# One load queue with casts on the engines, and head-major query features for eight 64x32 array tiles

**Chip, cores, metric.** One core of one Trainium2 chip. The metric is the device time of one execution in microseconds (us). A profiled execution also has a *span*, from the first to the last instruction, which lies about 2.1 us under the time. A ratio below is the mean time of one kernel's fast runs over that of the other's fast runs of the same rounds, so it is not quite the ratio of the medians quoted beside it; a "fast" run is one within about 1.5% of its kernel's fastest.

Names used throughout: PE is the tensor engine, PEld its weight loads, DVE the vector engine, ACT the scalar engine, POOL GpSimd, SP the engine that issues most transfers. In the traces, H holds `x @ w_in` before the silu (two buffers), G its silu (eight buffers), Vh a batch's values as bf16, `ot` a transposed block of the output. The "key-value products" of a batch are the `kv` of the reference, its "numerators" the `num`. A line of a profile's timeline gives start, duration, engine, line of the program, operation, tiles (written<-read), shapes, how many were merged, and in brackets the idle time before it and what ended it.

## The reference

Linear attention with quadratic features, then an expert layer with silu. 4 batches, 4 heads, 1088 positions, head dimension 32.

```python
def phi(x):                       # 8 x 8 = 64 features of each position
    a = np.einsum('rd,bhsd->bhsr', S1, x)
    b = np.einsum('rd,bhsd->bhsr', S2, x)
    return np.einsum('bhsi,bhsj->bhsij', a, b).reshape(*x.shape[:-1], 64)
kv  = einsum('bhsf,bhsd->bhfd', phi(k), v);  z = sum_s phi(k)
num = einsum('bhsf,bhfd->bhsd', phi(q), kv)
den = einsum('bhsf,bhf->bhs',  phi(q), z)[..., None] + 1e-06
x   = (num / den), heads side by side          # 4352 tokens x 128
h   = x @ w_in                                 # 128 -> 2048
out = (h * sigmoid(h)) @ w_out                 # 2048 -> 128
```

## The kernel before

The program is a list of small tasks. A constant `ORDER` says in which order they are emitted and, where a task may run on several engines, on which. Each engine works its own part of that list strictly in order, and SP issues its transfers strictly in order. So a place in the list is as much a part of the kernel as the instruction. What the change touches:

```python
def load_in(i):     # w_in, cast to bf16 by the GpSimd queue's transfer
    nc.gpsimd.dma_start(w_in[:, DFF // 2 * i: DFF // 2 * (i + 1)], moe_w_in[:, DFF // 2 * i: DFF // 2 * (i + 1)])
def load_out(i):    # w_out likewise
    nc.gpsimd.dma_start(w_out[:, 8 * i: 8 * (i + 1), :].rearrange(...), moe_w_out[...].rearrange(...))
gate = pl.add("POOL", 0.1, lambda: nc.gpsimd.tensor_copy(out=mark, in_=Kx[0][...]), ...)  # holds them back till keys 0 are in
...
def kvm():          # duplicate K'V and mask it, so that two heads share one 128-row product
    nc.vector.tensor_tensor(out=st["kvx"], in0=_bc(st["kvp"][:, 0: R * R], 0, 2), in1=_bc(pmask[:, :], 1, R * R), op=ALU.mult)
...
def num(sl):        # numerators: block-masked KV, whole 128x128 array, two head pairs accumulate
    for hp in range(2):
        nc.tensor.matmul(sl[:, :m], kst["KV"][:, hp, :], rhs, start=(hp == 0), stop=(hp == 1))
```

SP's order was: second half of queries 0, first half, values 0, keys 1, one piece of values 2, keys 2, a piece of values 1, queries 1, another piece of values 1 and so on. Two of the four pieces of values 2 stand behind the transposes of batch 1's query features.

Of the kernel before, what the change touches and what calls it, by code (L numbers as in the profile page):

```python
# [15 lines left out]
ORDER = """  # L16
7 0 64 6 18 19 1 2.1 3.0 23 24 20 21 22 12 25 27 26 4 5 14 13 15 40 8 45 65 46 49 48 41 42 43 66 69
68 47 50 57 67 16.0 30.0 31 32.0 33 36.0 17.0 38.0 39 51 37 52.0 53 54.0 34.1 35 28.1 29 44.1 55
56.0 58 59.0 60 61.0 87 10 95 94 219 220 222 70 71 72.0 62 63.1 96 98 97 9 225 11 221 223 224 228
135 73 226 227 229 131 138 77.1 74.0 233 234 78 79.1 230 231 236 237 104 80 102.0 91 92 112 75 105  # L20
76.1 90 235 139 239 106 81.0 240 242 243 107 175 183 113 116 114 115 117 247 250 100.0 103.0 99.0
238 241 244 118 119.0 248 249 253 132 89 251 252 256 245 254 232 88 136 140 142 141 257 93.0 177
101.0 255 123.1 259 260 108 148 149 258 262 263 182 109 110 144.0 261 265 120 111.0 121 143.0 266
268 269 264 150 122.1 273 274 267 276 277 156 270 271 82.1 83 84.0 151 279 280 246 124 125 126.1
282 283 184 157 186 185 159 146.0 299 302 300 133 180 134 179 158 272 303 145.0 147.0 137.0 152 192
189.0 160 161 162 305 306 163.0 285 286 275 127.1 278 281 288 289 164 178 284 308 85 86.1 309 287
167.0 168 311 312 301 314 315 304 307 191.0 317 318 171.0 172 153 154 310 291 292 187.1 313 294 295
155.0 165 166.1 320 321 316 319 193 325 326 290 328 329 293 194 188.1 200 331 195 128 332 296 297
334 335 169 170.1 337 338 176 322 323 201 340 341 343 204 298 344 181.0 203 324 202 190.0 196 351
205 352 206 207.0 208 327 330 197 354 355 333 336 357 358 339 360 361 353 129 130.1 363 364 356 366  # L30
198 342 369 367 370 359 372 373 199.0 209 210.1 346 347 362 173 174.1 377 378 211.1 212 345 380 365
215.1 216 381 217 218.1 383 384 348 386 387 379 389 390 213 403 404 368 382 392 393 371 406 407 374
385 395 396 388 398 349 350 399 391 409 410 394 214.1 417 418 375 376 397 420 421 400 401 402 412
413 405 408 423 424 411 431 432 414 415 416 426 427 419 434 435 422 437 438 425 428 429 430 440 441
433 436 439 442 443 444
"""
# [8 lines left out]
class Plan:  # L45
# [29 lines left out]
    def replay(self, seq):  # L75
        now, mode, queue, port = dict(self.now), None, 4.0 - 1.6, 0.0
        free = {k: [(i, 0.0) for i in range(len(v))] for k, v in self.slots.items()}
        for t, c in seq:
            eng, cost = t["eng"][c], t["cost"][c]
            at = max(now.get(eng, 0.0), t["ready"])  # L80
            for d in t["deps"]:
                at = max(at, d["done"] + d["lag"] + self.hop(d["on"], eng) * (d["dq"] == 0.0))
            got = []
            for pool in t["take"]:
                i, when = free[pool].pop(0)
                got.append(i)
                at = max(at, when)
            if eng == "PE":
                cost += self.MODE if mode not in (None, t["mode"]) else 0.0
                mode = t["mode"]  # L90
            if t["tt"] and eng in ("DVE", "POOL"):
                at = max(at, port)
                port = at + cost
            t["on"], t["start"], t["end"], t["got"] = eng, at, at + cost, got
            now[eng] = t["done"] = t["end"]
            if t["dq"]:
                queue = t["done"] = max(queue, t["end"]) + t["dq"]
            for u, i in t["give"]:
                free[u["take"][i]].append((u["got"][i], t["end"] + self.FREE))
# [19 lines left out]
def kernel(  # L119
# [11 lines left out]
    nc = tc.nc  # L131
# [78 lines left out]
    QTs = [const.tile([P, 4, CW], FP32, name=f"QT{i}") for i in range(2)]  # L210
    KVs = [const.tile([P, 2, P], BF16, name=f"KV{i}") for i in range(2)]
    AW = [const.tile([P, NBX * H, R + 1], FP32, name=f"AW{i}") for i in range(2)]
# [6 lines left out]
    identb = const.tile([P, P], BF16, name="identb")  # L219
    mark = const.tile([P, 1, 1], FP32, name="mark")  # L220
    warm = const.tile([P, 1], FP32, name="warm")
# [16 lines left out]
    for t in Vf:  # L238
        nc.vector.memset(t[64:, :, NB, :], 0.0)
    for t in KVs:  # L240
        nc.gpsimd.memset(t, 0.0)
    for t in AW:
# [45 lines left out]
    def key_tasks(b, cuts):  # L288
# [65 lines left out]
        def kvm0(eng):  # L354
            st["KV"] = KVs[b % 2]
            dst = AP(tensor=st["KV"].tensor, offset=st["KV"].offset, ap=[list(st["KV"].ap[0]), [P + 64, 2], [D, 2], [1, D]])
            src = H0[:, :, 0:64].rearrange("p q (g d) -> p q g d", g=2)
# [16 lines left out]

        def kvm():
            st["kvx"] = work.tile([P, 2, R * R], BF16, name="kvx", tag="kvx")
            nc.vector.tensor_tensor(out=st["kvx"], in0=_bc(st["kvp"][:, 0: R * R], 0, 2),
                                    in1=_bc(pmask[:, :], 1, R * R), op=ALU.mult)

# [4 lines left out]
        def kvc(eng):  # L384
            st["KV"] = KVs[b % 2]
            dst = AP(tensor=st["KV"].tensor, offset=st["KV"].offset, ap=[list(st["KV"].ap[0]), [P + 64, 2], [1, 64]])
            copy(eng, dst, st["kvb"].rearrange("p (q m) -> p q m", q=2))

# [15 lines left out]
        for i, (lo, hi) in enumerate(parts):  # L404
# [3 lines left out]
                         (st["pr"][-1:] if False else []) + ([st["lk"]] if b else []) + old,  # L408
                         ready=((3.5, 3.95), (4.5, 4.9))[i][c // 2] if b == 0 else 0.0, name=nm(f"kt{c}{lo}")) for c in (0, 2)]
            st["kt"] += k1  # L410
# [27 lines left out]
        if b == 0:  # L438
            st["kvd"] = pl.add(("DVE", "ACT"), (0.3, 0.44), kvm0, kvs, name=nm("kvm"))
            early.append(st["kvd"])  # L440
        else:
            k1 = pl.add("PE", 0.42, kv, ou + vc, take=("s",), mode="32", name=nm("kv"))
            t = pl.add("DVE", 0.29, kvm, [k1], name=nm("kvm"))
            t = pl.add("PE", 0.12, kvt, [t], name=nm("kvt"))
            st["kvd"] = pl.add(("DVE", "ACT"), (0.22, 0.3), kvc, [t] + ([qs[b - 2]["nums"]] if b >= 2 else []),
                               give=[(k1, 0)], name=nm("kvc"))
# [19 lines left out]
    def scale_cost(n):  # L466
        return 0.75 + 0.13 * n

    def back_end(b, o, lo, hi, pe):
# [40 lines left out]
        m = pl.add("PE", 0.05 + 0.107 * n, num, [c, kst["kvd"]], take=("s",), name=nm("num"))  # L510
        st["nums"] = m
        st[f"x{lo}"] = pl.add(both, (0.17 + 0.107 * n, 0.08 + 0.135 * n), xcopy, [m], give=[(m, 0)],
                              due=T0 + STEP * (16 * b + 12) if n == 1 else None, name=nm("x"))

    def query_tasks(b, spans, pe=False, groups=None):
# [57 lines left out]
        for g, (glo, ghi) in enumerate(groups):  # L573
# [7 lines left out]
            for lo, hi in spans:  # L581
                if lo < glo or hi > ghi:
                    continue
                o = pl.add(("DVE", "POOL"), (0.1 + 0.26 * (hi - lo), 0.08 + 0.52 * (hi - lo)),
                           lambda e, lo=lo, hi=hi: outer(e, lo, hi), [sc], tt=True, name=nm(f"outer{lo}"))
                back_end(b, o, lo, hi, pe)

    def store_main(b, a0, na, queues):
# [103 lines left out]
    def load_in(i):  # L692
        nc.gpsimd.dma_start(w_in[:, DFF // 2 * i: DFF // 2 * (i + 1)], moe_w_in[:, DFF // 2 * i: DFF // 2 * (i + 1)])

    def load_out(i):
        nc.gpsimd.dma_start(w_out[:, 8 * i: 8 * (i + 1), :].rearrange("p (i j) m -> p i (j m)", i=2),
                            moe_w_out[DFF // 2 * i: DFF // 2 * (i + 1), :].rearrange("(i p j) m -> p i (j m)", i=2, p=P))

    gate = pl.add("POOL", 0.1, lambda: nc.gpsimd.tensor_copy(out=mark, in_=Kx[0][:, KN[0] + KN[1] + KN[2] + CUT: KN[0] + KN[1] + KN[2] + CUT + 1, 0:1]), ready=4.9, due=4.0, name="gate")
    for i in range(2):  # L700
        win += [dma(524, lambda i=i: load_in(i), [gate], issue=0.75, lag=2.6, due=4.2 + 0.1 * i, eng="POOL", rate=400.0, name=f"lwi{i}")] * 2
    for i in range(2):
        wout += [dma(524, lambda i=i: load_out(i), [gate], issue=0.85, lag=2.6, due=4.5 + 0.1 * i, eng="POOL", rate=380.0, name=f"lwo{i}")] * 2

# [8 lines left out]
    for b in range(1, B):  # L713
        pl.floor = T0 + 1.0
        load(b)
        key_tasks(b, KCUT)
        query_tasks(b, [(0, 4), (4, 8), (8, 9)])
    pl.floor = None
    for b in range(B):
        for lo, hi in ((0, 2), (2, 4), (4, 8)) if b == 0 else (  # L720
                ((0, 4), (4, 6), (6, 8)) if b == B - 1 else ((0, 4), (4, 8))):
            if (b, lo) == (B - 1, 4):
                moe_tasks(xR.rearrange("p b x -> p (b x)"), B * XN, [qs[i]["x8"] for i in range(B)], store_rest, 8, tag="mR")
            need = [qs[b][f"x{i}"] for i in range(8) if f"x{i}" in qs[b] and lo <= i < hi]
            need = need or [qs[b][f"x{i}"] for i in range(8) if f"x{i}" in qs[b] and i <= lo][-1:]
            moe_tasks(xT[b][:, P * lo: P * hi], P * (hi - lo), need,
# [39 lines left out]
```

## Time and profile before

| | before |
|---|---|
| time, first comparison | median 102.04 us (101.77 to 104.64, 4 runs) |
| time, three later comparisons, 11 runs each | medians 102.18, 101.74, 101.53 us (99.72 to 105.32) |
| first expert matmul in the trace | 17.58 us (second trace 16.81) |
| ACT silu, 68 instructions | 64.8 us busy, 7.7 us idle in front of them |
| last output transpose starts | 93.10 us (second trace 94.46) |

### The profile page before, as it was taken

What the parts mean: (1) busy time and instruction counts of PE and PEld (TensorE: products, weight loads), DVE (VectorE), ACT (ScalarE), POOL (GpSimd) and SP (SyncE); (2) the same over time, 40 slices, a digit from 0 to 9 for tenths busy, and PEclk for the clock granted to TensorE, in tenths of its full rate; (3) what the DMA queues carried; (4) which work ended last, traced back from release to release, by engine and by line L of the source; (5) the groups of instructions that cost most, each with busy time, mean ns of one, the idle gap of its engine ahead of it and who ended that gap; (6) DMA issues with size and microseconds to landing.
All of it is one profiled execution on the core that took longest, in us unless ns stands there. A gap on an engine that the chain in (4) does not pass through costs nothing.

```text
span 98.6 us, 2224 instructions
## 1 busy us (share of the span) xinstructions
PE 89.5 (91%) x852; PEld 52.5 (53%) x852; DVE 54.7 (55%) x135; ACT 72.0 (73%) x89; POOL 33.4 (34%) x43
## 2 busy tenths in 40 slices
PE   5996999999999799978999999999999999999700
PEld 4543476798573445425445453554444556899500
DVE  4563779998799927689691848791123220211200
ACT  3330405889877569983999998979999999999400
POOL 6079800079409999139100071058000000000000
PEclk9999999999999999999999999999999999999995
DMA  2899999999973277990077303455700607062332
GB/s 52 230 294 260 203 150 178 300 263 268 150 236 105 52 125 140 320 162 0 0 160 133 86 0 57 74 89 105 134 3 0 109 5 106 4 103 33 47 49 31
DMA packets 30841, 11.87 MB, mean 120 GB/s; under 512 B 26224, under 2 KB 29552, under 8 KB 30832
## 3 DMA queue, kind: packets, MB, share of 16 engines
q1 hardware_dynamic: 29376, 10.62, 49.7%
q0 software_dynamic: 832, 1.05, 7.3%
q10 hardware_dynamic: 624, 0.07, 0.5%
q8 instruction: 6, 0.10, 0.4%
q14 instruction: 3, 0.02, 0.1%
HBM read 8.79 MB, written 2.23 MB: 112 GB/s over the span
## 4 chain that ended last, share of the span: by engine, by line
PE 52%; DMA 18%; DVE 14%; SPq 4%; POOL 4%; issue 2%; DVEq 0%
PE B L630 23%; PE H L619 21%; DMA Kx<-in_k_dram 8%; DMA Qx<-in_q_dram 6%; DMA Vf<-in_v_dram 4%; DVE qp L463 3%; POOL kp L321 2%; DVE KT L298 2%; PE B L497 2%; SPq L185 2%; PE B L267 1%; PE B L541 1%; POOL Vh L163 1%; DVE aqs L458 1%; SPq L189 1%
## 5 line engine op out<-in xcount | busy, mean ns | idle before, releaser
L623 ACT ACTIVATE G<-H 128x1024 bf16<-128x1024 f32 x68 | 64.8, 1035 | 7.7 <-PE H L619 6.3
L630 PE MATMUL B<-G,w_out 128*128 128x512 bf16 (+1 forms) x176 | 37.8, 331 | 0.0
L619 PE MATMUL H<-xT,w_in 128*128 128x512 bf16 (+1 forms) x160 | 37.5, 337 | 0.0
L619 PEld LDWEIGHTS <-w_in 128*128 128x128 bf16 x176 | 18.9, 115 | 12.2 <-issue 3.0
L630 PEld LDWEIGHTS <-w_out 128*128 128x128 bf16 x176 | 16.7, 98 | 10.0 <-issue 0.5
L321 POOL TENSOR_TENSOR kp<-kab 128x512 bf16<-128x512 f32 (+1 forms) x17 | 16.7, 999 | 0.4 <-DVE kab L315 0.2
L635 DVE STREAM_TRANSPOSE ot<-B 128x512 f32<-128x512 f32 (+1 forms) x11 | 6.5, 594 | 15.7 <-PE B L630 12.9
L463 POOL TENSOR_TENSOR qp<-aqs,qabm 128x256 bf16<-128x256 f32 (+2 forms) x6 | 9.3, 1559 | 13.8 <-DVE aqs L458 13.8
L733 PE MATMUL B<-zero 128*128 128x256 bf16 x42 | 8.8, 347 | 1.1 <-DVE fmask L229 1.1
L163 POOL CAST Vh<-Vf 128x1152 bf16<-128x1152 f32 x3 | 3.4, 1143 | 17.4 <-DMA Vf<-in_v_dram 17.4
L163 DVE CAST xT<-B 128x512 bf16<-128x512 f32 (+1 forms) x8 | 5.0, 619 | 6.4 <-PE B L497 6.3
L463 DVE TENSOR_TENSOR qp<-aqs,qabm 128x1024 bf16<-128x1024 f32 (+2 forms) x8 | 8.4, 1055 | 0.2
L298 DVE STREAM_TRANSPOSE KT<-Kx 128x512 f32<-128x512 f32 (+4 forms) x10 | 6.1, 614 | 1.9 <-DMA Kx<-in_k_dram 1.9
L733 PEld LDWEIGHTS <-zero 128*128 128x128 bf16 x42 | 4.6, 119 | 3.1 <-DVE fmask L229 1.1
L526 DVE STREAM_TRANSPOSE QT<-Qx 128x1024 f32<-128x1024 f32 (+1 forms) x5 | 5.0, 1020 | 2.0 <-DMA Qx<-in_q_dram 2.0
L497 PE MATMUL B<-qt,KV 128*128 128x512 bf16 (+2 forms) x28 | 5.8, 296 | 0.0
L161 ACT ACTIVATE qt<-B 128x512 bf16<-128x512 bf16 (+1 forms) x4 | 2.2, 544 | 3.4 <-PE B L484 3.4
L497 PEld LDWEIGHTS <-KV 128*128 128x128 bf16 x28 | 2.6, 98 | 2.6 <-ACT KV L360 0.2
L548 DVE STREAM_TRANSPOSE qabm<-B 128x288 f32<-128x288 f32 (+1 forms) x8 | 3.0, 418 | 0.7 <-PE B L267 0.6
L541 PE MATMUL B<-QT,WM 128*32 128x288 f32 (+2 forms) x40 | 3.3, 430 | 0.0
L161 ACT ACTIVATE Vh<-Vf 128x640 bf16<-128x640 f32 (+1 forms) x2 | 1.3, 674 | 2.5 <-DMA Vf<-in_v_dram 2.5
L163 DVE CAST xR<-B 128x64 bf16<-128x64 f32 x4 | 0.9, 225 | 3.9 <-PE B L497 3.9
(70 smaller groups left out, 63.5 us busy)
## 6 DMA issues: line engine op xcount, KB each, us to landing
Kx<-in_k_dram SPq DMA_DIRECT2D x3, 544.0 KB, 7.9
Qx<-in_q_dram SPq DMA_DIRECT2D x3, 544.0 KB, 4.5
out_dram<-ot SPq DMA_DIRECT2D x24, 64.0 KB, 2.0
Vf<-in_v_dram SPq DMA_DIRECT2D x8, 144.0 KB, 3.8
Vf<-in_v_dram SPq DMA_DIRECT2D x8, 128.0 KB, 5.7
w_in<-in_moe_w_in_dram POOLq DMA_DIRECT2D x2, 256.0 KB, 6.9
w_out<-in_moe_w_out_dram POOLq DMA_DIRECT2D x2, 256.0 KB, 5.9
out_dram<-ot SPq DMA_DIRECT2D x14, 32.0 KB, 1.7
```

Of the source, the lines that this page charges most:

```text
L163: eng.tensor_copy(out=out, in_=in_)
L298: nc.vector.transpose(out=KT[:, c:c + 2, 32 * lo: 32 * hi], in_=src.rearrange("p c a d -> p c (a d)"))
L321: eng.tensor_tensor(out=st["kp"][:, H * lo: H * hi], in0=_bc(a, 2, R), in1=_bc(bb, 1, R), op=ALU.mult)
L463: eng.tensor_tensor(out=st[f"qp{lo}"], in0=_bc(st["aqs"][:, H * lo: H * hi], 2, R), in1=_bc(bq.rearrange("p a (h r) -> p (a h) r", h=H), 1 ...
L497: nc.tensor.matmul(sl[:, :m], kst["KV"][:, hp, :], rhs, start=(hp == 0), stop=(hp == 1))
L526: nc.vector.transpose(out=QT[:, :, 32 * lo0: 32 * n].rearrange("p c (a s) -> p a c s", s=32), in_=Qx[b][:, 4 * lo0: 4 * n, :].rearrange("p ...
L541: nc.tensor.matmul(sl[32 * c: 32 * (c + 1), 32 * lo0: 32 * hi0], w, QT[:, c, 32 * lo0: 32 * hi0], start=True, stop=True, tile_position=(0, ...
L619: nc.tensor.matmul(view(sl, i), w_inj[:, (J * jp + i) // 4, (J * jp + i) % 4, :], x, start=True, stop=True)
L623: nc.scalar.activation(out=sl, in_=cc[jp], func=ACT.Silu)
L630: nc.tensor.matmul(cc["o"][:, :n], w_out[:, j, :], view(cc["g", jp], i), start=(j == 0), stop=(j == NJ - 1))
L635: nc.vector.transpose(out=cc["ot"][:, :n], in_=cc["o"][:, :n])
L733: nc.tensor.matmul(hold["bank"][:, 0:256], zero[:, 0:P], zero, start=True, stop=True)
```

## The change

The intent: take the weights' transfers away from GpSimd, put every load into one queue whose order can be chosen, and spend PE less on the numerators of batches 1 to 3 by laying their query features out head by head, so that eight small products stream at once. The core of the diff (the renumbered `ORDER`, the plan's costs and most of the new function are cut):

```diff
-    KVs = [const.tile([P, 2, P], BF16, name=f"KV{i}") for i in range(2)]
+    KV0 = const.tile([P, 2, P], BF16, name="KV0")
+    KVd = [const.tile([P, P], BF16, name=f"KVd{i}") for i in range(2)]
 ...
-        def kvm():
+        def kvm(eng):
             st["kvx"] = work.tile([P, 2, R * R], BF16, name="kvx", tag="kvx")
-            nc.vector.tensor_tensor(out=st["kvx"], in0=_bc(st["kvp"][:, 0: R * R], 0, 2),
-                                    in1=_bc(pmask[:, :], 1, R * R), op=ALU.mult)
+            copy(eng, st["kvx"], _bc(st["kvp"][:, 0: R * R], 0, 2))
 ...
+        def back(p):     # query features go to (head, block, feature) order, not (block, head, feature)
+            dst = st["abm"][:, 0:2, 0:NM].rearrange("p n (h a r) -> p a n h r", h=H, r=R)
+            nc.vector.transpose(out=dst[:, :, :, 2 * p: 2 * p + 2, :], in_=st["p"][p][:, 0:NM])
+            nc.vector.transpose(out=st["abm"][:, 0:2, NM + 2 * R * p: NM + 2 * R * (p + 1)], in_=st["p"][p][:, NM:CW])
 ...
+        def num(s0, s1):
+            st["n"] = [s0, s1]
+            for h in range(H):
+                for g in range(2):
+                    nc.tensor.matmul(st["n"][g][D * h: D * (h + 1), :], kst["KV"][64 * g: 64 * (g + 1), D * h: D * (h + 1)],
+                                     st["qt", h // 2][64 * g: 64 * (g + 1), 4 * (h % 2): 4 * (h % 2) + 4, :],
+                                     start=True, stop=True, tile_position=(64 * g, D * h))
 ...
     def load_in(i):
-        nc.gpsimd.dma_start(w_in[:, DFF // 2 * i: DFF // 2 * (i + 1)], moe_w_in[:, DFF // 2 * i: DFF // 2 * (i + 1)])
+        nc.sync.dma_start(w_inf[:, DFF // 2 * i: DFF // 2 * (i + 1)], moe_w_in[:, DFF // 2 * i: DFF // 2 * (i + 1)])
 ...
+    def cast_w(eng, dst, src, i):
+        copy(eng, dst[:, DFF // 4 * i: DFF // 4 * (i + 1)], src[:, DFF // 4 * i: DFF // 4 * (i + 1)])
```

The new list also moves other work: which engine forms which product, and which transfer goes first. SP now sends the first half of queries 0 first, and all of values 2 before it comes to the transposes of batch 1.

## The prediction

> **What bounds the kernel now.** I read the page's totals first, then the busy time by stretches, then the timeline around the first expert matmuls, then single places in the PE timeline where it changes its array mode.
>
> ```profile
> PE 89.5 (91%) x852; PEld 52.5 (53%) x852; DVE 54.7 (55%) x135; ACT 72.0 (73%) x89; POOL 33.4 (34%) x43
> ...
> L623 ACT ACTIVATE G<-H 128x1024 bf16<-128x1024 f32 x68 | 64.8, 1035 | 7.7 <-PE H L619 6.3
> L630 PE MATMUL B<-G,w_out 128*128 128x512 bf16 (+1 forms) x176 | 37.8, 331 | 0.0
> L619 PE MATMUL H<-xT,w_in 128*128 128x512 bf16 (+1 forms) x160 | 37.5, 337 | 0.0
> ```
>
> PE's 91% is not one limit: 8.8 us of it are matmuls on zeros that keep the clock up, and the ends are modelled. The row to hold on to is L623: 68 silu tiles cannot be had for less than 68 times the rate of a queue that never waits, and ACT lost 7.7 us in front of them, nearly all to PE. Busy time in three stretches (columns: us; then busy time and count of PE, PEld, DVE, ACT, POOL; clock; DMA share; GB/s):
>
> ```profile
> 17.50:45.00 27.50, 25.96 (x337) 15.66 (x334) 22.25 (x47) 22.95 (x28) 17.33 (x16) 1.00 0.81 188
> 45.00:66.30 21.30, 21.30 (x189) 10.47 (x174) 15.09 (x26) 18.28 (x20) 5.53 (x6) 1.00 0.37 69
> 66.30:92.40 26.10, 26.10 (x171) 17.05 (x170) 5.63 (x13) 25.28 (x27) 2.49 (x2) 1.00 0.35 58
> ```
>
> So there are four stages. **Until 17.5 us** nothing of the expert layer runs: the first head's features wait for data. **17.5 to 66 us** PE has too much to do: attention matmuls for later batches are threaded between expert matmuls and ACT idles (22.95 of 27.5, 18.28 of 21.3). **66 to 92.4 us** ACT is the limit (25.28 of 26.1; one piece of the timeline has 15 silu in 14.12 us, 0.94 each). **After that** a tail of some 6 us, the last products, transpose and store, which the change leaves alone. What is saved in stages 1 and 2 arrives at the end; what PE saves in stage 3 does not.
>
> The chain into stage 2, from the timeline (start, us, what):
>
> ```profile
> 8.90 1.30 DVE L526 STREAM_TRANSPOSE QT<-Qx 128x512 f32<-128x512 f32 x2 [1.75 <-DMA Qx<-in_q_dram]
> 11.14 1.25 ACT L161 ACTIVATE Vh<-Vf 128x640 bf16<-128x640 f32 x2 [2.49 <-DMA Vf<-in_v_dram]
> ...
> 14.80 0.75 DVE L321 TENSOR_TENSOR kp<-kab 128x256 bf16<-128x256 f32 x2
> ...
> 16.00 0.51 ACT L360 ACTIVATE KV<-H,fmask 128x64 bf16<-128x64 f32 x2
> ```
>
> DVE waits 1.75 us for the first queries (8.90), though the half that is wanted first is issued behind the other half; then the last two key products of batch 0 run on DVE (14.80) and KV is ready only at 16.5, the first product of numerators at 16.57, its copy at 17.0, the first expert matmul at 17.47.
>
> **What the Trainium skill says.** "DMA: Bandwidth & Descriptors", section "SWDGE vs HWDGE vs iDMA": a cast inside a DMA exists only on the GpSimd queue, so moving the weights to SyncE's queue must add cast instructions; its section "Issuing engines are not separate DMA queues" says all queues end in the same 16 engines and interleave. The trace agrees: with both queues live the DMA share is 1.0 and 7.4 to 17.3 us carry (260+203+150+178)x2.465 = 1.95 MB counted at the destination; the 1.05 MB of weights there are twice that at the source, so about 3.0 MB in 9.9 us, 303 GB/s, as with one queue alone (294 in the slice before). So I expect **no bandwidth gain**, only another order of arrival. "TensorEngine Tiling (Array Packing)", section "Key Properties": a change of tiling mode drains the array, and tiles run independently. The trace agrees, with this pair from the PE timeline:
>
> ```profile
> 59.82 0.59 PE L630 MATMUL B<-G,w_out 128*128 128x512 bf16 x2
> 60.34 0.72 PE L267 MATMUL B<-QT,WP 64*32 64x288 f32 x16
> 60.99 1.05 PE L619 MATMUL H<-xT,w_in 128*128 128x512 bf16 x4
> ```
>
> L630's two would let the next start at 60.25 (0.215 each); L267 starts 0.09 later. Two such sets back to back start 0.50 apart (40.88 and 41.38), so 0.48 to 0.50 is its streaming time, and L619 should start at 60.83 but does at 60.99. An excursion to 64x32 and back costs **0.25 us**. Third, "SBUF — State Buffer", section "Who interferes with whom": a DVE instruction with two SBUF inputs and a GpSimd instruction that reads SBUF block each other. The trace agrees roughly: POOL's products of 512 columns took as little as 1.07 us, so 1024 should take 2.1, but the one that started at 65.22 beside DVE's of 1.23 us took 2.96.
>
> **The change, part by part.**
>
> (1) *Loads.* The order on SyncE's queue becomes keys 0, first half of the queries, second half, values 0, keys 1, w_in, one w_out quarter, queries 1, then w_out quarters among batch 1 and 2 loads. The first query half takes the place of the one that landed at 2.8+4.7 = 7.5, so it lands near 7.3 instead of 8.9: 1.6 us early. DVE is then busy with a key product it took from POOL (0.7) until about 7.6, so the chain gets about 1.3 of it. A second key product (0.4) is put between; the two that delayed KV at 14.80 go to earlier places, +0.45 back. The cast of the first w_in quarter stands on ACT before the first x copy, about 0.1 net. Sum 1.3-0.4+0.45-0.1 = 1.25, and what PE and DVE no longer queue for adds a little: I put **first expert matmul at 16.0, -1.5 us**. Bytes ahead of w_in's first half: 0.56+0.26+0.30+0.56+0.56+0.52 = 2.76 MB; from the slices 0.47 MB are in by 4 us, then 270 GB/s: 12.5 to 13.5 us, before the 14.7 or so at which ACT wants it. w_out's first quarter (4.5 MB) comes near 20, its cast near 20.7; PE has eight H units, keys 1 and the rest of batch 0 until about then.
>
> (2) *Casts.* Eight of 512 columns. POOL's 1152-column cast took 1.14 us, so about 0.55 each: seven on POOL (3.9 us), one on ACT. POOL has room: 17.33 of 27.5 busy in stage 2, and loses two DMA waits. Cost on the path: none beyond the 0.1.
>
> (3) *Values come earlier.* Batch 2's values are now loaded by about 29 us. Before, the cast waited for them until 43.5:
>
> ```profile
> PE B L371 <- POOL Vh L163: 1.0, 1, 1.0
> ```
>
> and PE stood for 1.0 us in stage 2, ACT for 1.68 behind it. **-1.0 us**.
>
> (4) *Numerators.* Before, per batch of 1 to 3: four 128x512 products (4x0.215) and two of 64 columns (0.06) = 0.92. After: eight 64x32 tiles at once, one stream of 512 columns, 0.215 to 0.25, plus the excursion 0.25 = 0.5. The rests stand beside other 64x32 work or late. Gain 0.4 a batch; batch 3's falls in stage 3 and is worth nothing. **-0.7 us** for two batches.
>
> (5) *Given back.* Head-major transposes split off the last 32 columns: three more DVE instructions of about 0.1 per batch, 0.3, beside other work. ACT gets masks-free KV copies and x copies: 2.1 us of non-silu work in stages 2 and 3 become about 3.0. In stage 2 it has 7.6 us to spare; a little shows. **+0.2 us**.
>
> Sum: -1.5-1.0-0.7+0.2 = -3.0, so 102.2-3.0 = **99.2 us**.
>
> **Rivals.** *A: weights late.* If the queue runs at the 150 to 180 GB/s of the slices from 12 to 17 us, w_in's first half lands after 16 and w_out after 25; ACT stands in its own order behind the cast. For: one queue is strictly in order, and eight G buffers cap how far H can run ahead. Against: that slow figure is the cast queue counted at the destination. It would make 101 to 103. *B: DVE takes over in stage 2.* It is busy 22.25 of 27.5; the new order gives it both products of queries 1 and two more copies, and takes three query products away. A batch's numerators now need both halves transposed before x exists; if x1 comes after the 16 units of batch 0 are gone, PE starves. By summing durations I get both halves of x1 near 34 us (36.9 and 40.6 transposed and multiplied before), with PE through batch 0 near 37, so against; it would make 100 to 101.5. *C: the gains are larger*, if ACT reaches its limit much earlier: all 7.7 us of idle are the most that can be won; with 4 to 5 of them 97.
>
> **Range and chances.** The start is uncertain by 1 us, the stall by 0.5, the packing of stage 2 by about 1 either way. Range 97.2 to 101.2. Two per cent is 100.15; chances 0.68 faster, 0.29 same, 0.03 slower.
>
> **What would show it.** Right: first L619 at 15.5 to 16.5; POOL's casts over before each use and no wait on w_out on PE over 0.5; numerators as eight tiles lasting about 0.3 to 0.5 with 0.25 lost around them; no PE wait for Vh; ACT 0.94 per silu from about 62 us; last silu near 89. Wrong: first L619 at 17 or later with ACT waiting for w_in, or PE waiting for x1 or w_out at 20 to 40 us, or the start gained and then lost because ACT's idle grows in stage 2.

## The result

The changed kernel took **99.27 us** (median; 98.59 to 101.12, 4 runs) against 102.04: ratio 0.9715, 95% interval 0.9638 to 0.9792. Two later comparisons gave 0.9904 (0.9803 to 1.0004; medians 100.23 and 102.18) and 0.9874 (0.9791 to 0.9958; 100.55 and 101.53). The gain is real, but between 1 and 3%; the first comparison was the largest.

The profile after, first the totals that answer to those of before (same columns):

```profile
PE 86.8 (89%) x869; PEld 51.4 (53%) x879; DVE 57.6 (59%) x146; ACT 71.8 (74%) x88; POOL 29.7 (31%) x41
...
L722 ACT ACTIVATE G<-H 128x1024 bf16<-128x1024 f32 x68 | 65.0, 1031 | 8.7 <-PE H L718 3.0
L729 PE MATMUL B<-G,w_out 128*128 128x512 bf16 (+1 forms) x174 | 37.4, 330 | 2.3 <-POOL w_out L163 2.0
```

ACT idles *more* in front of the silu than before, 8.7 against 7.7 us, and PE has a new wait: 2.0 us for a cast of w_out on POOL. By stretches, cut at the same places as before:

```profile
17.50:45.00 27.50, 24.79 (x328) 14.47 (x332) 21.54 (x46) 20.76 (x29) 19.81 (x21) 1.00 0.83 172
45.00:66.30 21.30, 21.14 (x162) 10.11 (x164) 16.42 (x32) 20.49 (x23) 1.48 (x2) 1.00 0.42 86
66.30:92.40 26.10, 25.26 (x173) 16.38 (x173) 5.28 (x12) 23.71 (x26) 0.00 (x0) 1.00 0.34 56
```

ACT is busy 20.76 us in the first stretch (22.95 before) although it starts earlier, and 20.49 in the second (18.28 before). The chain into the expert layer, from the timeline:

```profile
7.55 1.41 DVE L524 STREAM_TRANSPOSE QT<-Qx 128x512 f32<-128x512 f32 x2
11.07 1.25 ACT L161 ACTIVATE Vh<-Vf 128x640 bf16<-128x640 f32 x2 [2.59 <-DMA Vf<-in_v_dram]
12.96 0.52 ACT L361 ACTIVATE KV<-H,fmask 128x64 bf16<-128x64 f32 x2 [0.64 <-issue]
15.22 1.04 PE L718 MATMUL H<-xT,w_in 128*128 128x256 bf16 x8
```

The queries are transposed at 7.55 (8.90 before) without a wait, KV starts at 12.96 (16.00), and the first expert matmul at 15.22 (17.58): the start comes 2.4 us earlier. And then, in the timeline of all engines:

```profile
27.13 3.31 DVE L638 TENSOR_TENSOR qp<-aqs,qabm 128x1024 bf16<-128x1024 f32 x2
27.21 2.15 POOL L163 CAST Vh<-Vf 128x1152 bf16<-128x1152 f32 x1 [2.09 <-DMA Vf<-in_v_dram]
29.31 1.60 POOL L163 CAST w_out<-w_outf 128x512 bf16<-128x512 f32 x1
30.96 1.05 PE L729 MATMUL B<-G,w_out 128*128 128x256 bf16 x8 [1.98 <-POOL w_out L163]
```

POOL waits till 27.21 for batch 1's values, its cast of them takes 2.15 us (1.14 before), the w_out cast queued behind takes 1.60 (0.61 elsewhere in this trace), and PE stands 1.98 us. All this lies beside two DVE products with two inputs in SBUF. One after another, the two products (2.36 in a later run where they were undisturbed), 1.14 and 0.61 would take 4.1 us, an estimate; from 27.13 to 30.91 are 3.8. So the four ran nearly one at a time. The second trace of the changed kernel has neither the early start (16.68) nor this wait, yet it ends at the same time.

**Two milestones** show where the gain is. The key-value products of batch 1 and of batch 2 are 36 small matmuls each, easy to find. Between them both kernels do the same amount of expert work on PE: 14 pairs of 128x512 matmuls in either trace (where PE records were missing, the pairs were completed from their weight loads). From the timeline of PE, two traces of before, then two of after (batch 1, batch 2):

```profile
33.25 0.56 PE L371 MATMUL B<-kp,Vh 128*32 128x64 bf16 x36 [0.35 <-DVE ot L635]
44.70 0.56 PE L371 MATMUL B<-kp,Vh 128*32 128x64 bf16 x36 [1.01 <-POOL Vh L163]
```
```profile
34.11 0.56 PE L371 MATMUL B<-kp,Vh 128*32 128x64 bf16 x36
46.06 0.56 PE L371 MATMUL B<-kp,Vh 128*32 128x64 bf16 x36 [1.52 <-POOL Vh L163]
```
```profile
33.67 0.56 PE L372 MATMUL B<-kp,Vh 128*32 128x64 bf16 x36
43.18 0.60 PE L372 MATMUL B<-kp,Vh 128*32 128x64 bf16 x36
```
```profile
33.59 0.56 PE L372 MATMUL B<-kp,Vh 128*32 128x64 bf16 x36
43.10 0.59 PE L372 MATMUL B<-kp,Vh 128*32 128x64 bf16 x36
```

Put together with the start of the first expert matmul and of the last output transpose:

| trace | first expert | to batch 1's products | to batch 2's | to the last transpose |
|---|---|---|---|---|
| before | 17.58 | 33.25 | +11.45 | +48.40 = 93.10 |
| before, second | 16.81 | 34.11 | +11.95 | +48.40 = 94.46 |
| after | 15.22 | 33.67 | +9.51 | +48.52 = 91.70 |
| after, second | 16.68 | 33.59 | +9.51 | +48.51 = 91.61 |

Up to batch 1's products nothing is gained, whatever the start. Between the two milestones 1.9 to 2.4 us are gained. After them the times are equal.

**The work is not, outside the middle.** Counted by the weight loads of the expert matmuls (352 in each trace), both traces of before have 80 of them behind them at batch 1's products and 108 at batch 2's, both traces of the changed kernel 78 and 106. The middle is equal, but the changed kernel is one pair of matmuls (0.43 us) further back at both milestones and does that pair afterwards. So up to batch 1's products it lost about 0.85 us between the first traces and gained 0.1 between the second, and after batch 2's it gains some 0.3 us in the same 48.5. Of the 68 silu, 22 have started at batch 2's products in before and 20 in the changed kernel, which so runs two more of them in that time. The starts of the same silu by number, in us:

| silu | before | before, second | after | after, second | mean lead of after |
|---|---|---|---|---|---|
| 1 | 18.22 | 17.45 | 15.86 | 17.31 | 1.25 |
| 20 | 41.33 | 42.17 | 42.41 | 42.33 | -0.62 |
| 23 | 46.34 | 47.70 | 45.78 | 45.71 | 1.28 |
| 37 | 60.14 | 61.50 | 59.95 | 59.87 | 0.91 |
| 42 | 66.32 | 67.68 | 64.73 | 64.64 | 2.31 |
| 68 | 91.39 | 92.75 | 89.58 | 89.49 | 2.53 |

For ACT the lead is gone by the 20th silu, comes back around batch 2's products and grows once more between the 37th and the 42nd, at 60 to 66 us. No run was made for that second step.

### The profile page after: what moved, and what is told of

Same layout as the page of the kernel before. It is cut to its first block, busy times and chain, and to the rows that moved or that the text cites. A ratio compares the mean times of both kernels' runs of the same rounds, so it can differ in the third digit from the quotient of the medians.

```text
span 97.4 us, 2280 instructions
## 1 busy us (share of the span) xinstructions
PE 86.8 (89%) x869; PEld 51.4 (53%) x879; DVE 57.6 (59%) x146; ACT 71.8 (74%) x88; POOL 29.7 (31%) x41
## 4 chain that ended last, share of the span: by engine, by line
PE 60%; DMA 20%; DVE 4%; POOL 4%; SPq 3%; issue 2%; ACT 2%; POOLq 0%; DVEq 0%; ACTq 0%
PE B L729 28%; PE H L718 25%; DMA Vf<-in_v_dram 8%; DMA w_outf<-in_moe_w_out_dram 7%; DMA Qx<-in_q_dram 5%; POOL Vh L163 2%; SPq L185 2%; POOL w_out L163 2%; ACT G L722 2%; PE B L372 1%; PE B L606 1%; PE B L650 1%; DVE qabm L546 1%; PE B L328 1%; DVE kp L322 1%
## 5 line engine op out<-in xcount | busy, mean ns | idle before, releaser
L638 DVE TENSOR_TENSOR qp<-aqs,qabm 128x1024 bf16<-128x1024 f32 (+1 forms) x8 | 8.8, 1136 | 0.1
L299 DVE STREAM_TRANSPOSE KT<-Kx 128x576 f32<-128x576 f32 (+4 forms) x10 | 6.0, 613 | 2.4 <-DMA Kx<-in_k_dram 2.3
L322 DVE TENSOR_TENSOR kp<-kab 128x512 bf16<-128x512 f32 (+1 forms) x6 | 4.5, 766 | 0.1
L594 DVE STREAM_TRANSPOSE QT<-Qx 128x1024 f32<-128x1024 f32 x3 | 3.7, 1233 | 0.9 <-DMA Qx<-in_q_dram 0.9
L462 POOL TENSOR_TENSOR qp<-aqs,qabm 128x512 bf16<-128x512 f32 (+1 forms) x4 | 3.8, 958 | 0.8 <-DVE aqs L457 0.8
L163 POOL CAST w_out<-w_outf 128x512 bf16<-128x512 f32 x4 | 3.4, 856 | 1.0 <-DMA w_outf<-in_moe_w_out_dram 1.0
L268 PE MATMUL B<-QT,WP 64*32 64x288 f32 (+1 forms) x64 | 3.3, 385 | 0.5 <-DVE WM L340 0.5
L316 DVE STREAM_TRANSPOSE kab<-B 128x288 f32<-128x288 f32 x6 | 2.5, 452 | 1.0 <-PE B L268 1.0
L618 DVE STREAM_TRANSPOSE qabm<-B 128x256 f32<-128x256 f32 x6 | 2.5, 420 | 0.8 <-PE B L268 0.8
L163 POOL CAST w_in<-w_inf 128x512 bf16<-128x512 f32 x3 | 1.9, 644 | 2.9 <-DMA w_inf<-in_moe_w_in_dram 2.9
```

The lines of the kernel that those rows point to most:

```text
L163: eng.tensor_copy(out=out, in_=in_)
L268: nc.tensor.matmul(dst[p][32 * c: 32 * (c + 1), lo:hi], WPf[64 * p: 64 * (p + 1), :], srcT[64 * p: 64 * (p + 1), c, lo:hi], start=True, st ...
L299: nc.vector.transpose(out=KT[:, c:c + 2, 32 * lo: 32 * hi], in_=src.rearrange("p c a d -> p c (a d)"))
L322: eng.tensor_tensor(out=st["kp"][:, H * lo: H * hi], in0=_bc(a, 2, R), in1=_bc(bb, 1, R), op=ALU.mult)
L462: eng.tensor_tensor(out=st[f"qp{lo}"], in0=_bc(st["aqs"][:, H * lo: H * hi], 2, R), in1=_bc(bq.rearrange("p a (h r) -> p (a h) r", h=H), 1 ...
L594: nc.vector.transpose(out=QT[:, :, 0: 32 * NB].rearrange("p c (a s) -> p a c s", s=32), in_=Qx[b][:, 0: 4 * NB, :].rearrange("p (a c) d -> ...
```

## The experiments

Twelve kernels ran, in three groups, each group on one chip with 11 runs of before beside it. Some profiled executions fell in a stretch of low granted clock; those are named, and only what lies outside that stretch is used from them. Edits of `ORDER` are given by the tasks' names: lq, lk, lv are loads of queries, keys, values (then the batch, then the piece; v0 is all pieces of values 0, lqa and lqb the halves of queries 0), lwi and lwo the loads of w_in and w_out, cwi and cwo their casts; in the rest the first letter and digit are the batch, with vcast for the cast of values, outer for feature products, dmat for their transposes, tr and st for the transpose and store of outputs, s for a silu.

### The same two kernels again

> The unchanged kernel before, for a second trace: the first trace of before has a span of 98.6 us, though its timed runs lie near 102 and the changed kernel's runs show a span some 2.1 us under the time, which would put before's usual span near 99.8. If the first trace was a quick execution, this one has a span of 99.3 to 100.3 and its first expert matmul or the middle stage is up to 1.2 us later; if the offset differs between the kernels, the span is 98.4 to 98.9 again.

The kernel before, unedited. Span 100.0 us: the first trace was a quick one. The start was earlier (16.81, in spite of the low clock from 11 to 15 us), the loss came later. PE waited 1.9 us for w_out's transfer and 1.5 us for batch 2's values.

> The unchanged changed kernel, for a ratio on this chip beside the other runs and a second trace. Theory: ratio 0.970 plus or minus 0.008, first expert matmul at 15.1 plus or minus 0.4 us, and again a wait of PE on the last cast of w_out of about 2 us near 29 us. If that wait was an accident of one execution it will be under 0.7 us here.

The changed kernel, unedited. 100.23 us, ratio 0.9904: outside the range I gave. First expert matmul 16.68, no wait on a cast; PE waited 1.3 us for an output transpose on DVE at 32.6 instead. The cast wait comes and goes, and another wait takes its place.

### One half of the change at a time

> Before, with one part of the change: all loads on the one hardware queue, first query half ahead of the second, weights as float32 with eight casts (one on ScalarE, seven on GpSimd), w_out's quarters placed ahead of batch 2's keys; the rest of the order, the query path and the engines of the products stay as before. Theory that the loads give the earlier start: first expert matmul at 16.0 to 16.7 and ratio 0.975 to 0.990. Rival that the engines' new order, not the loads, gives it: first expert matmul at 17 or later and ratio 0.992 to 1.005. Rival that the weights come late for the old order, which wants w_out at 19.9: PE waits over 1 us on w_out's casts and the ratio is over 1.0.

```diff
 kernel before, with load_in, load_out and cast_w of the changed kernel
-SP: lqb lqa v0 lk1 lv23 lk2 lv13 lq1 lv12 lk3 lv20 ...     POOL: gate lwi0 .. lwo0 lwi1 lwo1 (casting transfers)
+SP: lqa lqb v0 lk1 lwi0 lwi1 lwo0 lwo1 lq1 lwo2 lwo3 lk2 v1 lq2 v2 lk3 ...   POOL: cwi1-3, cwo0-3; ACT: cwi0
```

103.79 us, ratio 1.0198 (1.0055 to 1.0341; the profiled run had a low clock from about 34 to 38 us). The loads alone make the old order **slower**, and the first expert matmul came at 18.51, later than before. The timeline of this kernel, DVE then POOL, shows one reason:

```profile
14.50 1.58 DVE L322 TENSOR_TENSOR kp<-kab 128x256 bf16<-128x256 f32 x2
16.00 0.63 DVE L456 TENSOR_TENSOR AW<-qabm 128x64 f32<-128x64 f32 x1
...
14.40 1.41 POOL L163 CAST w_in<-w_inf 128x512 bf16<-128x512 f32 x2 [0.69 <-DMA w_inf<-in_moe_w_in_dram]
15.83 1.28 POOL L163 CAST w_out<-w_outf 128x512 bf16<-128x512 f32 x2
```

The two key products took 0.75 us before and take 1.58 beside POOL's casts; AW took 0.22 and takes 0.63. The casts that I called free beside other work slow DVE's products on the very chain that leads to the start. DVE also waited 5.4 us for a key transfer here, which my queue order had put behind the weights; the two causes aren't separated in the time.

> The changed kernel with the other part undone: weights again cast by the GpSimd queue's transfers, in four pieces at the places they had, no cast instructions; query path, numerators, the hardware queue's order and the engines' order as in the changed kernel. Theory that the loads give the earlier start of about 2.2 us and the cast of w_out takes 2.0 us back at 29 us: first expert matmul at 16 to 17, no wait on a cast, ratio within 0.012 of the changed kernel's (0.965 to 0.985). Rival that the single queue is worth more than that because it keeps keys and values from being delayed: ratio 0.985 to 1.0. Rival that the casts cost more than the queue gains: ratio under 0.965.

```diff
 changed kernel, with load_in, load_out, gate of the kernel before; casts gone
-SP: ... lk1 lwi0 lwi1 lwo1 lq1 lv22 lwo0 lk2 ...
+SP: ... lk1 lq1 lv22 lk2 ...          POOL: gate lwi0 (k0 products) lwo0 lwi1 lwo1, casting transfers
```

99.67 us, ratio 0.9823 (0.9694 to 0.9953), against 0.9904 for the whole change on the same chip. First expert matmul 16.44; milestones 33.37 and 42.88; end 91.36. **The gain is there without any of the single weight queue.** Moving the weights and casts is not what makes the kernel faster; the rest of the change is: query path, numerators, and the order of the other loads and engines. No run separates these from each other as wholes: the new query layout in the old order, or the old layout in the new order, was not built.

### The values of batch 2

> Before, with one move in the hardware queue's order: the third and fourth piece of batch 2's values go out right behind the second, some 19 us, instead of behind the transposes of batch 1's queries at 38 us. Theory that most of the gain is that PE no longer waits for these values: the PE wait on the cast values (1.0 and 1.5 us in two traces) is gone, ScalarE's silu waits between 45 and 70 us fall from 3.2 to 3.7 to under 2.2, and the ratio is 0.980 to 0.992. Rival that the gain is the numerators' and the new engine order's: the wait goes but the ratio is 0.993 to 1.005.

```diff
 kernel before
-SP: ... lv20 lv11 m00st lv10 lq2 lv31 q1dmat0 m02st q1dmat4 lv21 lq3 lv22 ...
+SP: ... lv20 lv21 lv22 lv11 m00st lv10 lq2 lv31 q1dmat0 m02st q1dmat4 lq3 ...
```

101.45 us against 101.74, ratio 1.0011 (0.9927 to 1.0095): as a time, no gain. The wait on the values was gone and ACT's silu waits between 45 and 70 us fell to 2.4 us. But the profiled run lost clock between 36 and 40 us, and PE waited 1.3 us before batch 1's products, which then came at 35.55. By the time alone the rival holds, that this wait by itself isn't worth much in the old order.

> The changed kernel, with the same two pieces of batch 2's values sent late again, behind batch 3's values at about 38 us, and their cast behind them on GpSimd. Theory: PE waits about 1 us for the cast values near 43 us, ScalarE loses 1 to 2 us more between 40 and 50 us, and the time is 1 to 2 us over the changed kernel's of the same chip. Rival: the wait comes but the time is within 0.5 us of it, since ScalarE is the limit afterwards anyway.

```diff
 changed kernel
-SP: ... lk2 lv21 lv10 ... lk3 lv20 lv23 q1dmat1 q1dmat0 m00st m02st lv31 lv30 lv32 lv33 ...    POOL: ... k2vcast k2outer0 ...
+SP: ... lk2 lv10 ... lk3 lv23 q1dmat1 q1dmat0 m00st m02st lv31 lv30 lv32 lv33 lv21 lv20 ...   POOL: ... k2outer8 k2vcast ...
```

102.83 us (before 101.74 on that chip; only one of its six runs was fast, so there is no ratio, and no run of the changed kernel there, so the gap in time to it is not known). The trace, PE's timeline:

```profile
41.69 0.69 PE L606 MATMUL B<-QT,WM 128*32 128x288 f32 x8
45.25 0.56 PE L372 MATMUL B<-kp,Vh 128*32 128x64 bf16 x36 [2.87 <-POOL Vh L163]
```

Batch 1's products had come at 32.69, so the step to batch 2's is 12.56 us, 3.05 more than the changed kernel's 9.51, with a wait of 2.87. The low clock in this run (46 to 50 us) comes after. From there to the last transpose it took 50.12, 1.6 more than usual, which is the size of that clock loss: four pairs of matmuls in it took 0.80 to 0.86 each for 0.43. So the wait was not given back later. **In the changed order** a wait on these values goes through to the end.

### What the numerators cost, and whether PE time counts late

> The changed kernel, with batch 2's numerators computed eight times over, the same values into the same place: 56 more tile matmuls of 64x32 by 512 columns. If eight tiles really stream at once each repeat is 0.215 us, so PE has 1.5 us more in the middle stage near 52 us, and the time rises by 0.8 to 1.6 us. Rival that the tiles share one stream: each repeat 0.86 us or more, 6 us in all, and the time rises by 4 us or more.

> The same eightfold repeat for batch 3's numerators, near 70 us, where ScalarE is the limit. Theory that PE time is worth nothing there: the time rises by 0 to 0.5 us over the changed kernel. Rival that PE still is the limit in that stage: it rises as much as with batch 2, 0.8 to 1.6 us.

```diff
 changed kernel (b is 2 in the first, 3 in the second)
-            for h in range(H):
+            for h in [i % H for i in range(H * 8)]:      # for that batch only
                 for g in range(2):
```

102.21 and 101.34 us (before 101.74 on that chip), ratios to before 1.0148 (1.0060 to 1.0236) and 1.0088 (1.0001 to 1.0175), spans of the profiled runs 99.0 and 98.5. PE's timeline of the first, then the numerators of the second:

```profile
51.52 0.59 PE L718 MATMUL H<-xT,w_in 128*128 128x512 bf16 x2
52.04 1.94 PE L650 MATMUL B<-qt,KVd 64*32 64x512 bf16 x64
53.91 0.62 PE L718 MATMUL H<-xT,w_in 128*128 128x512 bf16 x2
```
```profile
69.56 1.92 PE L650 MATMUL B<-qt,KVd 64*32 64x512 bf16 x64
71.41 0.62 PE L718 MATMUL H<-xT,w_in 128*128 128x512 bf16 x2
```

From 52.04 to 53.91 are 1.87 us. Once only, it is 52.70 to 53.09, 0.39 (below). Seven repeats so take 1.48, **0.21 us each: eight tiles do stream at once.** The way from batch 2's products to the last transpose grew from 48.5 to 50.50 with batch 2's repeat (which also saw a 0.5 us wait for a transposed block) and to 49.96 with batch 3's. So my statement that PE time is worth nothing once ACT is the limit is **refuted** for a block of this size: here 1.85 less 0.39 us, 1.46 us of PE near 70 us, cost 1.46. ACT's silu waits after 70 us rose from 0.4 to 1.8. In the changed kernel a block of some 0.5 us there (0.39 and the change of mode) costs no visible wait, and the whole of what the repeat adds does, so only about 0.5 us are absorbed. That the two H buffers set this limit is argued, not shown. The rival named above, that PE still is the limit there, fits as well: two pairs for each silu take PE 0.86 us, and silu mostly start 0.90 to 0.92 apart.

### What meters the stretch up to batch 1's products

> The changed kernel once more, as the reference for the three below on this chip. Ratio to before 0.97 to 0.995; first expert matmul anywhere from 15.0 to 16.8 us, yet the key-value products of batch 1 again at 33.4 to 33.8 us whatever the start, if the theory holds that vector and GpSimd engines, locked against each other from 27 to 33 us, meter the kernel there.

Unedited again: ratio 0.9874. Here PE waited 2.0 us on the w_out cast once more. The profiled run lost clock from 32 to 35 us and its batch 1 products came at 35.88, so it says nothing on the theory.

> The changed kernel with one cast moved: the last quarter of w_out is cast by ScalarE, which idles there, instead of GpSimd behind the values of batch 1. Theory (the cast matters only when it falls in the locked stretch): PE waits on a cast under 0.3 us in place of 0.7 to 2.0, GpSimd has 0.6 to 1.6 us less in the stretch, the key-value products of batch 1 start 0.5 to 1.0 us earlier, time 0.3 to 1.0 us lower than the changed kernel's. Rival: PE merely waits on something else in the same place (the output transposes on the vector engine) and the time is within 0.3 us.

```diff
 changed kernel
-POOL: ... cwo2 k1vcast cwo3 k1outer2 ...            ACT: ... m04s1 m04s2 ...
+POOL: ... cwo2 k1vcast k1outer2 ...                 ACT: ... m04s1 cwo3 m04s2 ...
```

**98.94 us** (98.08 to 100.12), ratio to before 0.9748 (0.9679 to 0.9816); the changed kernel beside it had 0.9874, so 0.9748/0.9874 = 0.987 of it. By its median it is the fastest kernel, and clearly faster than before; the intervals of the two ratios still overlap a little, so its lead over the changed kernel is probable, not shown. (Its four fast runs, 98.08 to 99.04, do all lie below the changed kernel's four beside it, 99.28 to 100.64.) From the timeline of its slowest execution, the one that was profiled (100.12 us), DVE, ACT, PE:

```profile
28.75 4.19 DVE L638 TENSOR_TENSOR qp<-aqs,qabm 128x1024 bf16<-128x1024 f32 x2
...
29.98 0.62 ACT L161 ACTIVATE w_out<-w_outf 128x512 bf16<-128x512 f32 x1
...
33.35 1.02 PE L729 MATMUL B<-G,w_out 128*128 128x512 bf16 x4 [0.79 <-DVE ot L734]
```

The cast costs 0.62 us on ACT, though it runs beside the same DVE products, and PE no longer waits for it. The stretch in which DVE and POOL slow each other is still there (DVE's two products 4.19 us), and PE waits 0.79 for the output transposes behind them. The trace itself started late (17.26), so its batch 1 products came at 34.31, not earlier as I had expected, and its last transpose at 92.31 (91.70 and 91.61 in the two traces of after). So this one trace shows the wait gone, but not where the 1.3% of the times comes from.

> The kernel with the changed query path and the weights on the GpSimd queue (query_only before), with the hardware queue sending the four pieces of batch 1's values ahead of batch 2's. Theory: these values land near 25 instead of 27.4 us, GpSimd casts and multiplies before the vector engine starts its two query products at 28 us, the lock is avoided, the key-value products of batch 1 start at 31 to 32.5 us, and the time is 0.5 to 1.5 us lower than the changed kernel's by more than query_only's 0.6. Rival: the values land earlier but the stretch stays as long, time within 0.4 us of query_only's place (0.3 to 0.9 us under the changed kernel).

```diff
 the query-only kernel
-SP: ... lq1 lv22 lk2 lv21 lv10 lv12 lv13 lv11 lq2 ...
+SP: ... lq1 lk2 lv10 lv12 lv13 lv11 lv22 lv21 lq2 ...
```

100.98 us, ratio 0.9917 (0.9833 to 1.0002), no better than the changed kernel's 0.9874 on that chip. The overlap was avoided as planned: batch 1's values were cast at 23.83, and DVE's two products took 2.36 us instead of 3.3 to 4.2. But PE had waited 1.4 us for w_in, DVE's products only started at 29.31, and batch 1's products came at 33.41. The expectation of 31 to 32.5 failed.

> The kernel of the run before this one, and on the vector engine the two output transposes of batch 0 are put between the two query products of batch 1 instead of behind both. Theory: PE's wait on the output transposes (0.9 to 1.3 us near 32 us) goes, time a further 0.3 to 0.8 us lower. Rival: the vector engine then waits for the outputs before the second query product and the time does not fall, or rises by up to 0.5 us.

```diff
 the kernel of the run before this
-DVE: ... q1outer1 q1outer0 m00tr m02tr ...
+DVE: ... q1outer1 m00tr m02tr q1outer0 ...
```

100.25 us, ratio 0.9903 (0.9845 to 0.9962): by the fast runs no gain over the run before it, though I had expected 0.3 to 0.8 us. The wait on the output transposes was gone. The first expert matmul came at 14.81, the earliest of all traces, and then (the view of PE's waits; columns: sum, count, longest):

```profile
PE H L716 <- DMA w_in<-in_moe_w_in_dram: 3.4, 1, 3.4
```

The second half of w_in arrives late through the casting queue, PE stands 3.4 us, and batch 1's products come at 33.38. In these two runs the lead was spent waiting for a weight.

**Taken together.** Where no low clock came before it, batch 1's products start at 33.37 to 33.67 us in five traces (after twice, query-only and its two variants), with first expert matmuls anywhere from 14.81 to 16.79. In values-late and the two with repeated numerators they start at 32.69 to 32.74, with first expert matmuls from 14.89 to 16.79; these three ran on one chip, another than the later four of the five, and the two with repeats are the changed kernel unedited up to that point. So about 1 us here differs by chip or by execution. Neither group follows its start. (The run with the cast on ACT, which started latest, at 17.26, has them at 34.31.) Different waits absorb the lead: the w_out cast, the output transposes, w_in's transfer. What the common meter is, in one resource, these runs don't settle; the contention of DVE and POOL, which I had named, was taken away in the first variant of query-only, and the milestone stayed.

## Why the prediction was right, and where not

The number was right (99.2 against 99.27), the sum behind it only in part; errors of opposite sign cancelled, so the closeness is luck. The later comparisons gave about 1%, not 3%. Two of the signs of being wrong that the prediction names did appear: the start was gained and then lost, and PE waited for w_out at 29 us.

1. **First expert matmul at 16.0, -1.5 us.** The event was forecast about right: 15.22, 16.68 and 16.35 in three traces, against 17.58 and 16.81; the mean is 16.08, 1.1 earlier, and two of the three lie outside the 15.5 to 16.5 that it named. Its worth was not: at batch 1's products the lead is 0 (33.67 and 33.59 against 33.25 and 34.11), or, by the work done, between 0.85 lost and 0.1 gained. The failed step is "What is saved in stages 1 and 2 arrives at the end". The wait on w_out that I put under 0.5 us was 2.0 in two of the three traces. It was a wait for the cast: the last quarter's transfer was issued at 18.81, such transfers landed in 7.4 to 9.0 us, and POOL came to its cast at 29.31.
2. **No bandwidth gain.** Right to about 5%. The prediction estimated 303 GB/s at the source over 9.9 us from 7.4 us on. The same four slices after (2.435 us each: 210, 366, 404, 295) carry 3.1 MB, 319 GB/s; in the second trace 317. The single slice of 404, while w_in's rows of 4 KB come in, shows an uneven rate, not a higher one on the whole. Rival A, late weights from a slow queue, did not come: the cast of w_in began at 13.43 where the prediction had its first half in by 12.5 to 13.5, and in the three traces of the changed kernel PE shows no wait for w_in.

```profile
GB/s 42 245 285 210 366 404 295 319 219 227 312 227 128 111 84 145 116 81 32 0 146 129 197 7 96 119 55 140 85 0 0 12 99 105 0 79 62 28 81 28
```

3. **Casts without cost.** Wrong in size and in place. Not 0.55 us but 0.61, and up to 1.60 beside DVE's products with two inputs; and they slow DVE's products as well (the loads-only run). Moving one cast to ACT gave about 1.3% of the time, with intervals that still overlap. The prediction quotes the rule that such instructions block each other, with a POOL product as its example (2.96 there is the mean of two; the one at 65.22 took 2.99), and then adds up the casts as if POOL were alone.
4. **Values come earlier, -1.0 us.** The wait is gone in every trace of the changed order but values-late's; it had been 1.01 and 1.52. Sending the values late again put 2.9 us in that place and 3.05 into that step. The same move alone in the old order gave no time, so the runs fit a gain that needs the rest of the order, though the times of the two runs alone don't show that.
5. **Numerators, -0.7 us for two batches.** The instruction cost was right: 0.5 forecast, and between the matmuls around it

```profile
52.17 0.59 PE L718 MATMUL H<-xT,w_in 128*128 128x512 bf16 x2
52.70 0.46 PE L650 MATMUL B<-qt,KVd 64*32 64x512 bf16 x8
53.09 0.62 PE L718 MATMUL H<-xT,w_in 128*128 128x512 bf16 x2
```

   the next pair could have started at 52.60 and starts at 53.09, 0.49. Batch 1's saving (0.86 to 0.44, from 36.40 to 36.84) lies between the milestones: with the 1.01 of the wait and 0.12 of a transpose pair that moved to later, that names 1.55 of the 1.94 us between the first traces; 0.39 stay unnamed. For the others I forgot what the new order splits: keys 3 no longer share an excursion with queries 3, the remainders of queries 2 and 3 make one of their own. After the second milestone before makes two excursions from the full array, the changed kernel six; four more at 0.25 are 1.0 us, an estimate, against about 1.35 saved. That would leave some 0.3, which fits 48.4 us before against 48.5 after with one pair more; no run took these excursions away, so it is argued, not shown.
6. **PE is worth nothing in stage 3.** Refuted for a block of 1.5 us, as above. And "17.5 to 66 us" was taken as one stage, without a term for its last part, where ACT gained once more at 60 to 66 us.

So the failed term is the start, sized at -1.5 and worth 0; the terms sized too small are those between the milestones, -1.0 and some -0.35, which together came to -1.9 to -2.4, and some -0.3 of PE's work after them. Rival B, that DVE takes over in the second stage, "100 to 101.5", described the later comparisons better than my centre did (100.23 and 100.55), though its mechanism, DVE's own load, is not shown: DVE and POOL were seen in each other's way, and taking that away left the milestone where it was.

## What to carry to other kernels

An earlier start is only worth what the next milestone shows: pick two or three events that both kernels must pass, check that the same work lies between them, before the first and after the last (here it did only between them), and compare the distances; gains and losses that cancel in the total come apart at once. When work moves to an engine that the traces show slowing another (here POOL and DVE), count it in the stretch where both are busy, and try first an engine that they show undisturbed (ACT's cast took 0.62 us in that stretch too). Compare rates over the same stretch, not a peak with a mean. And a save of streaming time by array tiles must be charged with every change of mode that the new order splits off, not only its own.

## What the Trainium skill lacked or had wrong

- "TensorEngine Tiling (Array Packing)", section "Key Properties": says that a change of mode drains the array, without a size. Here a way to 64x32 and back cost about 0.25 us beyond the streaming, and a whole set of eight 64x32 tiles of 512 columns 0.44 to 0.49 us between full-array matmuls, 0.21 us of it streaming.
- "SBUF — State Buffer", section "Who interferes with whom": it calls the shared port pair an exclusive lock. The traces agree nearly (the four instructions above in 3.8 us, 4.1 one after another) and add sizes: a POOL cast of 1152 columns 1.14 us alone and 2.15 beside DVE products, one of 512 columns 0.61 and 1.60; a pair of DVE products 2.36 us undisturbed and up to 4.19.
- No page that I read says how long PE may be away from two H buffers before ACT waits: here some 0.5 us cost nothing visible, and 1.46 more cost 1.46.
